# Two attention forms and a phase mixer on one core: paired tails, one more transpose by DMA, copies moved between engines, and a new order of work

## The chip, the cores and the metric

The kernel runs on one core of a Trainium2 chip. The core has TensorE (PE, matrix products), VectorE (DVE), ScalarE (ACT), GpSimd (POOL) and SyncE (SP), which here only issues DMA transfers. The metric is the device time of one execution in microseconds. The kernel before takes 247.88 us as the median of three runs (247.21 to 248.44). The profiled execution has a span of 247.0 us from its first to its last instruction.

## The reference

There are 8 batches, 8 heads, 576 positions and 64 elements per head; the model width is 512. Each batch has an attention over means of four positions, an attention over the seven positions around each one, and then a mixer whose phases come from a product with `w_theta`.

```python
q_d, k_d, v_d = means over 4 neighbouring positions of q, k, v
out_d = softmax(q_d k_d^T / 8) v_d               # 144 x 144, each row repeated 4 times
attn  = softmax(q k^T / 8 where |i - j| < 4)     # 576 x 576, a band
x     = repeat(out_d, 4) + attn v                # then the heads side by side: 576 x 512

theta = x @ w_theta                              # 512 x 512
zr, zi = x * cos(theta), x * sin(theta)
y     = w_tok_r @ zr + w_tok_i @ zi              # 576 x 576, over positions
u     = x + y
out   = u + max(u @ w_ch, 0)                     # 512 x 512
```

## The kernel before

The work of a batch is cut into steps, each a generator, and each step has a letter. The string `ORDER` says in which sequence the program takes them, over all batches; every engine runs its instructions in the order so given. L and v load, C and w cast to bf16, A turns q and k, Q and S form the two kinds of scores, N and V the products with v, T turns the result into xT, H forms the phases, Z multiplies x by cosine and sine, X mixes over positions, R multiplies by `w_ch`, O adds and stores. q, t, x, z and u issue DMA transposes. D are matmuls on zeros that keep TensorE at work.

The 576 positions of a batch are 4 blocks of 128 and a tail of 64.

```python
DMA_QK, DMA_X, DMA_Z = (6, 7), (6, 7), (6, 7)    # batches whose q/k, attention result, x are turned by DMA

def turns(b):                                    # step A; j = q, k, q, k
    for j in range(4):
        if b in DMA_QK:
            ps = turned.pop((b, j)).rearrange("p r w -> p (r w)")      # SBUF, written by a DMA transpose
        else:
            ps = w2(...)                                               # PSUM
            for r in range(WR):                                        # WR = 9
                nc.tensor.transpose(out=ps[:, P * r:P * r + P], in_=tm[:, i, r, :, :], identity=ident)
        for a in range(2):
            act(                                                       # nc.scalar.copy
                out=To[:, 2 * i + a, 0:S].rearrange("p (w r) -> p w r", r=WR),
                in_=ps.rearrange("p (r a w) -> p a w r", r=WR, a=2)[:, a],
            )
        # ... VectorE: tensor_reduce over four positions, to qdT or kdP
```

In these copies the output is written consecutively, and the input is read with a step of 128 elements.

```python
def turn_z(b):                                   # step x
    if b in DMA_Z:
        t = turned[b, "z"] = moep.tile([P, 16, P], BF16, tag="xr", bufs=1, ...)
        nc.sync.dma_start_transpose(out=t, in_=xTs[b][:, 0:4 * MAIN])

def modulate(b):                                 # step Z
    for c in range(4):
        if b in DMA_Z:
            ps = turned[b, "z"][:, c:16:4, :]
        else:
            for dc in range(4):
                nc.tensor.transpose(out=ps[:, dc, :], in_=xA[:, dc, P * c:P * c + P], identity=ident)
        nc.vector.tensor_tensor(out=z[:, 2 * c:2 * c + 2, :]..., in0=ps..., in1=css..., op=ALU.mult)

def mix(b):                                      # step X: psu four times, then psut for the tail
    uT = uTs[b] = moep.tile([P, 4 * S], BF16, tag="uT", ...)
    uA, uB = parted(uT)                          # main blocks and tail in one tile
    for dc in range(4):
        for j in range(9):
            nc.tensor.matmul(out=ps, lhsT=z[:, j, P * dc:P * dc + P], rhs=WT[:, j, 0:MAIN], ...)
        nc.vector.tensor_tensor(out=uA[:, dc, :], in0=ps, in1=xA[:, dc, :], op=ALU.add)
    # ... psut: 36 matmuls of 64 columns, and one addition into uB

def u_turn(b):                                   # step u, twice a batch: ur (main), utr (tail)
    nc.sync.dma_start_transpose(out=ur, in_=uTs[b][:, 0:4 * MAIN])
    nc.sync.dma_start_transpose(out=utr, in_=uTs[b][:, 4 * MAIN:4 * S])

def channels(b):                                 # step R, five times a batch
    # c < 4: four matmuls 128 x 512 into psr; c == 4, the tail of 64 positions:
    for dc in range(4):
        for hf in range(2):
            nc.tensor.matmul(out=psr[64 * hf:64 * hf + 64, 0:256], lhsT=uB[:, dc, :], rhs=wch[...][:, hf], ...)

def store(b):                                    # step O, five times a batch
    osb = moep.tile([P, DM], FP32, tag="osb", bufs=4, ...)
    nc.vector.scalar_tensor_tensor(out=osb..., in0=psr..., scalar=0.0, in1=ur or utr, op0=ALU.max, op1=ALU.add)
    # c < 4: one transfer of 128 rows; c == 4: two transfers of 64 x 2 pieces of 128 floats
```

Four PSUM buffers serve psu, psut, psth, psr and the other small products (`w1`), two larger ones the scores and the products with v (`w2`).

Of the kernel before, what the change touches and what calls it, by code (L numbers as in the profile page):

```python
# [10 lines left out]
BF16 = mybir.dt.bfloat16  # L11
AF = mybir.ActivationFunctionType
ALU = mybir.AluOpType
AX = mybir.AxisListType

P = 128
B = 8
H = 8
S = 576
# [15 lines left out]
WR = 9  # L35
# [6 lines left out]
HALF = 64  # L42
MAIN = 512
# [4 lines left out]
def kernel(  # L48
# [11 lines left out]
    nc = tc.nc  # L60
# [5 lines left out]
    moep = ctx.enter_context(tc.tile_pool(name="moep", bufs=2))  # L66
# [6 lines left out]
    def w2(name, dt=FP32):  # L73
        return ps2.tile([P, 2, 512 if dt == FP32 else 1024], dt, tag="w2" + next(turn2), name=name)

    def w1(name, dt=FP32):
        return ps1.tile([P, 512 if dt == FP32 else 1024], dt, tag="w1" + next(turn1), name=name)


    ORDER = (  # L80
        "LKLLLLLKKCLCCAvCCLvCDwvvvKLCAACwwwwLASCLSVQQCBlLLLLLVSlllllNvlCCCCNlvvvACNVCcScwcvTlTTccllcwAASlHVVH"
        "wwwDTTcAHZHZcHSZcccSDDhLLLzBcCSCWQDVWWLghLLLLCWCCvQvWWLNCNCCWWSWvvLvZNVVXwwwvAAvhwhTXTAALXSwSLLLLXQQ"
        "TBCCVgLggHCuLLVTvHNTVHHZNCCHCCCSwzZZZARRvvvSwOROALSXOLLAAXLLwSwwLvCCCCSCCCCRSNVOXVVXQVTTTAABwSXuTLLA"
        "vvwuvQRvvLLSTSHONNHVLLXuZZANHCLwHwwLVVHRQRRCCCCOzvLLLBOOCCSSTZTCvvRwOTLZSQHVHNVTXTAAXLLACACwCHHwCLCq"
        "LwwqNVHXSZNVXZZvvzSLLCCQCLqXVZLqQvRvwBvOVTVuTTLXTAwASSCHCCHCHNNXqvLwwTwuVXLVLAAHHXqSSZXRQROzONZSCCQC"
        "TCZBSVqROqvvvvZTSSROTVHVRHOTNNTXAAHVHHVwwwwwXAtAXSSzXXSSZZNZVuRuuRRROOQQtOOBRVRVttROtTTTOZOSTNXVRTuN"
        "RRxSSOOOHHVVXtttVHZHZZHNVzZXXttXuXTTXXHTHTTRxROOZHHRuROOHZRZZzOXXXXXXXRuRRRuuOORRuOOROROOORROO"
    )

    staged = {}  # L90
# [86 lines left out]
    for i in range(2):  # L177
        t = const.tile([P, 4, 5, KP], BF16, name=f"kdP{i}")
# [4 lines left out]
    for i in range(2):  # L183
        t = const.tile([P, 4, 5 * 120], BF16, name=f"kT{i}")
# [4 lines left out]
    for i in range(2):  # L189
        t = const.tile([P, NCH, H, 66], BF16, name=f"v_w{i}")  # L190
# [4 lines left out]
    for c in range(NCH):  # L195
        t = const.tile([P, DM], BF16, name=f"tmp{c}")
# [4 lines left out]
    for i in range(2):  # L201
        t = const.tile([P, 2, H, 66], BF16, name=f"vd{i}")
# [7 lines left out]
    dve, act, gp = nc.vector.tensor_copy, nc.scalar.copy, nc.gpsimd.tensor_copy  # L210
# [4 lines left out]
    wch = wpool.tile([P, 4, DM], BF16, name="wch")  # L215
# [69 lines left out]
    parts, turned = {}, {}  # L285


    DMA_QK, DMA_X, DMA_Z = (6, 7), (6, 7), (6, 7)

    def turn_qk(b):  # L290

# [23 lines left out]
    def turns(b):  # L315

        q_tm, k_tm = inputs.pop(b)
        qT = work.tile([P, 4, S], BF16, tag="qT", name=f"qT{b}")
        kT = kTs[b % 2]
        qdT = work.tile([P, 4, SD], BF16, tag="qdT", name=f"qdT{b}")  # L320
        kdP = kdPs[b % 2]
        parts[b] = (qT, kT, qdT, kdP)

        for j in range(4):
            n, i = j % 2, j // 2
            tm, To = ((q_tm, qT), (k_tm, kT))[n]
            if b in DMA_QK:
                ps = turned.pop((b, j)).rearrange("p r w -> p (r w)")
            else:
                ps = w2(f"pstr{n}{i}_{b}", BF16).rearrange("p k e -> p (k e)")[:, 0:WR * P]  # L330
                for r in range(WR):
                    nc.tensor.transpose(out=ps[:, P * r:P * r + P], in_=tm[:, i, r, :, :], identity=ident)  # L332
            for a in range(2):
                act(  # L334
                    out=To[:, 2 * i + a, 0:S].rearrange("p (w r) -> p w r", r=WR),
                    in_=ps.rearrange("p (r a w) -> p a w r", r=WR, a=2)[:, a],
                )
            hs = slice(2 * i, 2 * i + 2)
            dst, src = (qdT[:, hs, :], qT[:, hs, :]) if n == 0 else (kdP[:, hs, :, 0:30], kT[:, hs, :])
            src = src.rearrange("p e (m j) -> p e m j", j=4) if n == 0 else src.rearrange("p e (g m j) -> p e g m j", g=5, j=4)  # L340
            with nc.allow_low_precision(reason="sums are taken in float32 and rounded once"):
                nc.vector.tensor_reduce(out=dst, in_=src, axis=AX.X, op=ALU.add)  # L342
            yield
# [177 lines left out]
    def parted(t):  # L521

        return (t[:, 0:4 * MAIN].rearrange("p (e t) -> p e t", e=4),
                t[:, 4 * MAIN:4 * S].rearrange("p (e t) -> p e t", e=4))
# [85 lines left out]
            yield  # L610


    uTs, urs = {}, {}

    def mix(b):

        (xA, xB), z = parted(xTs[b]), zs.pop(b)
        uT = uTs[b] = moep.tile([P, 4 * S], BF16, tag="uT", name=f"uT{b}")
        uA, uB = parted(uT)
        for dc in range(4):  # L620
            ps = w1(f"psu{dc}_{b}")
            for j in range(9):
                nc.tensor.matmul(out=ps, lhsT=z[:, j, P * dc:P * dc + P], rhs=WT[:, j, 0:MAIN], start=(j == 0), stop=(j == 8))  # L623
            nc.vector.tensor_tensor(out=uA[:, dc, :], in0=ps, in1=xA[:, dc, :], op=ALU.add)  # L624
            yield
        ps = w1(f"psut_{b}")[:, 0:4 * HALF].rearrange("p (e t) -> p e t", e=4)
        for dc in range(4):
            for j in range(9):
                nc.tensor.matmul(out=ps[:, dc, :], lhsT=z[:, j, P * dc:P * dc + P], rhs=WT[:, j, MAIN:S],  # L629
                                 start=(j == 0), stop=(j == 8))  # L630
        nc.vector.tensor_tensor(out=uB, in0=ps, in1=xB, op=ALU.add)
        yield

    def u_turn(b):

        ur = moep.tile([P, 16, P], BF16, tag="ur", name=f"ur{b}")
        utr = moep.tile([P, 2, P], BF16, tag="utr", name=f"utr{b}")
        urs[b] = ur, utr
        nc.sync.dma_start_transpose(out=ur, in_=uTs[b][:, 0:4 * MAIN])
        yield  # L640
        nc.sync.dma_start_transpose(out=utr, in_=uTs[b][:, 4 * MAIN:4 * S])
        yield

    rels = {}

    def channels(b):

        uA, uB = parted(uTs[b])
        for c in range(5):
            psr = rels[b, c] = w1(f"psr{c}_{b}")  # L650
            if c < 4:
                for dc in range(4):
                    nc.tensor.matmul(  # L653
                        out=psr, lhsT=uA[:, dc, P * c:P * c + P], rhs=wch[:, dc, :],
                        start=(dc == 0), stop=(dc == 3),
                    )
            else:

                for dc in range(4):
                    for hf in range(2):  # L660
                        nc.tensor.matmul(  # L661
                            out=psr[64 * hf:64 * hf + 64, 0:256], lhsT=uB[:, dc, :],
                            rhs=wch[:, dc, :].rearrange("p (j e d) -> p e j d", j=2, e=2)[:, hf],
                            start=(dc == 0), stop=(dc == 3),
                        )
            yield

    def store(b):

        ur, utr = urs.pop(b)  # L670
        for c in range(5):
            psr = rels.pop((b, c))
            osb = moep.tile([P, DM], FP32, tag="osb", bufs=4, name=f"osb{c}_{b}")
            n = 4 if c < 4 else 2
            nc.vector.scalar_tensor_tensor(  # L675
                out=osb[:, 0:P * n].rearrange("p (e d) -> p e d", d=P),
                in0=psr[:, 0:P * n].rearrange("p (e d) -> p e d", d=P), scalar=0.0,
                in1=ur[:, c:16:4, :] if c < 4 else utr, op0=ALU.max, op1=ALU.add,
            )
            if c < 4:  # L680
                nc.sync.dma_start(out=out[b, P * c:P * c + P, :], in_=osb)
            else:
                for hf in range(2):
                    nc.sync.dma_start(  # L684
                        out=out[b, 512:576, :].rearrange("t (j e d) -> e t j d", j=2, e=2)[hf],
                        in_=osb[64 * hf:64 * hf + 64, 0:2 * P].rearrange("p (j d) -> p j d", j=2),
                    )
            yield

    last = {}
# [13 lines left out]
    def batches(steps):  # L709
        for b in range(B):  # L710
            yield from steps(b)

    sequences = dict(L=batches(load), v=batches(load_v), C=batches(cast), w=batches(cast_v), A=batches(turns), B=batches(pooled_v), Q=batches(scores), S=batches(band_scores), N=batches(pooled_out), q=batches(turn_qk), t=batches(turn_x), x=batches(turn_z),
                     V=batches(outputs), T=batches(transposes), H=batches(phases), Z=batches(modulate),
                     K=constants(), z=batches(z_turn), u=batches(u_turn), X=batches(mix), R=batches(channels), O=batches(store),
                     l=weight_loads(), c=weight_casts(), h=channel_loads(), g=channel_casts(), W=weight_turns(), D=warm_up())
    pin()
# [35 lines left out]
```

## Time and profile before

| | |
|---|---|
| time, median of 3 | 247.88 us |
| span of the profiled execution | 247.0 us |
| TensorE busy | 224.8 us, 91% |
| VectorE busy | 184.6 us, 75% |
| ScalarE busy | 166.9 us, 68% |
| GpSimd busy | 160.9 us, 65% |
| DMA queue of SyncE, share of 16 engines | 93.3% |
| mean granted clock of TensorE | 0.985 |

A line of the profile's groups names the line of the program, the engine, the operation, output and input by the program's names with partitions x elements, the count, busy time and mean ns of one, and the idle time before them with what ended most of it. Matmuls overlap, so the mean of one is longer than what a further one adds; the chain of waits, which gives the time that a run of matmuls takes on the path, is better for that. A line of the timeline gives start, duration, engine, program line, operation and count.

### The profile page before, as it was taken

To read this page: it belongs to the slowest core of one execution; us is meant where nothing else is said; L and a number is where in the kernel's file an instruction comes from. 1 tells how busy PE (TensorE), PEld (TensorE's weight loads), DVE (VectorE), ACT (ScalarE), POOL (GpSimd) and SP (SyncE) were. 2 spreads that over 40 slices of the span, in tenths; PEclk is the share of its full clock that TensorE was granted. 3 is DMA by queue.
4 is the path that set the end of the run, shared out by engine and by line. 5 is a ranking of instruction groups with operands and counts; after the bars stand their busy time and mean duration, and the time that the engine had idled before them with its cause. 6 is when DMAs were issued, how large, how long until landed. Compare 5 with 4: busy or idle time off the path is not lost. (4 is left out here: it accounts for less than half of the span.)

```text
span 247.0 us, 6608 instructions
## 1 busy us (share of the span) xinstructions
PE 224.8 (91%) x2602; PEld 134.9 (55%) x2602; DVE 184.6 (75%) x345; ACT 166.9 (68%) x248; POOL 160.9 (65%) x223
## 2 busy tenths in 40 slices
PE   0778799999999999999999998999699999999990
PEld 0435465765566566656666555655455655455540
DVE  5274976679879898897989977997687776256462
ACT  3685799766998479988878999899924390250000
POOL 4467485997999999979759664996295942400000
PEclk9997999999999999999999999999989999999999
DMA  6999999999979997999999999599969594946496
GB/s 197 307 272 391 304 211 330 333 224 245 275 200 275 320 197 122 263 239 314 256 185 214 252 184 269 92 172 219 121 156 169 144 209 96 170 160 90 90 262 202
DMA packets 100511, 53.94 MB, mean 218 GB/s; under 512 B 83968, under 2 KB 86016, under 8 KB 100480
## 3 DMA queue, kind: packets, MB, share of 16 engines
q1 hardware_dynamic: 100480, 53.53, 93.3%
q8 instruction: 20, 0.33, 0.6%
q14 instruction: 11, 0.09, 0.2%
HBM read 33.59 MB, written 9.44 MB: 174 GB/s over the span
## 5 line engine op out<-in xcount | busy, mean ns | idle before, releaser
L623 PE MATMUL psu<-WT,z 128*128 128x512 bf16 x288 | 66.3, 379 | 0.5 <-ACT cs L568 0.5
L445 POOL TENSOR_SCALAR_AFFINE_SELECT pm<-pm 128x1024 bf16<-128x1024 bf16 (+1 forms) x35 | 36.6, 1045 | 20.0 <-ACT pm L438 20.0
L438 ACT ACTIVATE pm<-psS 128x1024 bf16<-128x1024 f32 (+1 forms) x40 | 37.7, 979 | 12.7 <-PE psS L430 11.9
L623 PEld LDWEIGHTS <-z 128*128 128x128 bf16 x288 | 26.8, 98 | 29.2 <-issue 0.8
L447 POOL TENSOR_SCALAR_AFFINE_SELECT pm<-pm 128x1024 bf16<-128x1024 bf16 (+1 forms) x35 | 36.6, 1045 | 2.4
L562 PE MATMUL psth<-wth,xT 128*128 128x512 bf16 x128 | 31.5, 379 | 0.1
L624 DVE TENSOR_TENSOR uT<-psu,xT 128x512 bf16<-128x512 f32 x32 | 21.8, 687 | 12.7 <-PE psu L623 12.6
L653 PE MATMUL psr<-wch,uT 128*128 128x512 bf16 x128 | 31.2, 383 | 0.0
L567 ACT ACTIVATE cs<-psth,pihc 128x512 bf16<-128x512 f32 x32 | 22.3, 697 | 11.8 <-PE psth L562 11.3
L131 POOL CAST v_w<-st_v 128x512 bf16<-128x512 f32 (+1 forms) x40 | 23.9, 614 | 9.2 <-DMA st_v<-in_v_dram 9.1
L511 DVE TENSOR_TENSOR tmp<-psloc,rl 120x512 bf16<-120x512 f32 (+2 forms) x40 | 27.6, 691 | 1.4
L342 DVE TENSOR_REDUCE qdT<-qT 128x288 bf16<-128x1152 bf16 x16 | 21.5, 1347 | 8.2 <-ACT qT L334 8.2
L675 DVE SCALAR_TENSOR_TENSOR osb<-psr,ur 128x512 f32<-128x512 f32 x32 | 21.6, 686 | 7.3 <-PE psr L653 6.7
L342 DVE TENSOR_REDUCE kdP<-kT 128x300 bf16<-128x1200 bf16 x16 | 22.3, 1397 | 5.8 <-ACT kT L334 5.8
L124 POOL CAST k_tm<-st_k 128x576 bf16<-128x576 f32 x32 | 21.5, 673 | 4.5 <-DMA st_k<-in_k_dram 4.3
L124 POOL CAST q_tm<-st_q 128x576 bf16<-128x576 f32 x28 | 18.7, 667 | 2.5 <-PE pstr L332 1.3
L334 ACT COPY qT<-pstr 128x576 bf16<-128x576 bf16 x24 | 14.2, 646 | 8.7 <-PE pstr L332 8.7
L545 DVE TENSOR_TENSOR xT<-xTps,xdT 128x480 bf16<-128x480 bf16 (+3 forms) x36 | 18.7, 548 | 0.9 <-PE xTps L541 0.7
L568 ACT ACTIVATE cs<-psth 128x512 bf16<-128x512 f32 x32 | 19.4, 606 | 0.0
L653 PEld LDWEIGHTS <-uT 128*128 128x128 bf16 x128 | 11.5, 99 | 12.2 <-issue 0.8
L430 PE MATMUL psS<-qT,kT 64*128 64x128 bf16 (+1 forms) x320 | 15.0, 220 | 3.1 <-ACT pm L438 2.2
L502 PEld LDWEIGHTS <-pm 128*128 128x128 bf16 (+1 forms) x320 | 14.9, 105 | 5.0 <-issue 0.7
(92 smaller groups left out, 390.2 us busy)
## 6 DMA issues: line engine op xcount, KB each, us to landing
st_q<-in_q_dram SPq DMA_DIRECT2D x32, 288.0 KB, 4.7
st_k<-in_k_dram SPq DMA_DIRECT2D x32, 288.0 KB, 5.0
st_v<-in_v_dram SPq DMA_DIRECT2D x32, 256.0 KB, 5.4
out_dram<-osb SPq DMA_DIRECT2D x32, 256.0 KB, 3.1
st_v<-in_v_dram SPq DMA_DIRECT2D x8, 192.0 KB, 4.8
tok<-in_moe_w_tok_r_dram SPq DMA_DIRECT2D x4, 288.0 KB, 7.6
tok<-in_moe_w_tok_i_dram SPq DMA_DIRECT2D x4, 288.0 KB, 4.2
th<-in_moe_w_theta_dram SPq DMA_DIRECT2D x2, 512.0 KB, 7.1
```

The lines of the kernel that those rows point to most:

```text
L124: eng[i](out=dst[:, hh // 2, :, hh % 2, :], in_=staged.pop((b, f"{'qk'[i]}{hh}")).rearrange("p (r d) -> p r d", d=D))
L131: gp(out=v_ws[b % 2][0:KW[c], c, :, 0:D], in_=staged.pop((b, f"v{c}"))[0:KW[c], 0:DM].rearrange("p (h d) -> p h d", d=D))
L342: nc.vector.tensor_reduce(out=dst, in_=src, axis=AX.X, op=ALU.add)
L438: nc.scalar.activation(out=pv, in_=ps[0:kw].rearrange("p e (j w) -> p (e j) w", w=P)[:, :, 0:qn], func=AF.Exp, scale=SCL,)
L445: nc.gpsimd.affine_select(out=pv, in_=pv, compare_op=ALU.is_ge, fill=0.0, base=off, pattern=[[0, 8], [-1, qn]], channel_multiplier=1)
L447: nc.gpsimd.affine_select(out=pv, in_=pv, compare_op=ALU.is_ge, fill=0.0, base=6 - off, pattern=[[0, 8], [1, qn]], channel_multiplier=-1)
L511: nc.vector.tensor_tensor(out=tmp[0:cnt].rearrange("p (e j d) -> p e j d", e=2, j=4), in0=pv[0:cnt, :, :, 0:D], in1=rl[0:cnt].unsqueeze(3) ...
L562: nc.tensor.matmul(out=th, lhsT=xA[:, dc, P * c:P * c + P], rhs=wth[:, dc, :], start=(dc == 0), stop=(dc == 3),)
L567: nc.scalar.activation(out=cs[:, 0, :], in_=th, func=AF.Sin, bias=pihc, scale=1.0)
L623: nc.tensor.matmul(out=ps, lhsT=z[:, j, P * dc:P * dc + P], rhs=WT[:, j, 0:MAIN], start=(j == 0), stop=(j == 8))
L624: nc.vector.tensor_tensor(out=uA[:, dc, :], in0=ps, in1=xA[:, dc, :], op=ALU.add)
L653: nc.tensor.matmul(out=psr, lhsT=uA[:, dc, P * c:P * c + P], rhs=wch[:, dc, :], start=(dc == 0), stop=(dc == 3),)
```

## The change

It has four parts. The tails of two batches (64 positions each) are put side by side into one tile, so that one block of 128 positions serves both in step R and in the DMA transpose, and one addition on VectorE serves both in step O. Batch 5's x, which TensorE turned for step Z, is turned by DMA as those of batches 6 and 7 are. For batches 6 and 7, whose q and k are turned by DMA, the copies of k go to VectorE, and ScalarE's copies of q run over the elements in the other order: consecutive reads and spaced writes. And the order of the steps is a new one throughout. The aim is to take matmuls off TensorE and copies off ScalarE.

```diff
     ORDER = (
-        "LKLLLLLKKCLCCAvCCLvCDwvvvKLCAACwwwwLASCLSVQQCB...        (694 steps)
+        "KKLLLLCCCCLAALLLvCCvvKCKDwvvLLLCLLLLAALSwwwSwlVVCB...    (683 steps)
     )
 ...
-    DMA_QK, DMA_X, DMA_Z = (6, 7), (6, 7), (6, 7)
+    DMA_QK, DMA_X, DMA_Z = (6,7),(6,7),(5,6,7)
 ...
             for a in range(2):
-                act(
-                    out=To[:, 2 * i + a, 0:S].rearrange("p (w r) -> p w r", r=WR),
-                    in_=ps.rearrange("p (r a w) -> p a w r", r=WR, a=2)[:, a],
-                )
+                dst = To[:, 2 * i + a, 0:S].rearrange("p (w r) -> p w r", r=WR)
+                src = ps.rearrange("p (r a w) -> p a w r", r=WR, a=2)[:, a]
+                if b not in DMA_QK:
+                    act(out=dst, in_=src)
+                elif n == 0:
+                    act(out=dst.rearrange("p w r -> p r w"), in_=src.rearrange("p w r -> p r w"))
+                else:
+                    dve(out=dst, in_=src)
 ...
-        uT = uTs[b] = moep.tile([P, 4 * S], BF16, tag="uT", name=f"uT{b}")
-        uA, uB = parted(uT)
+        uT = uTs[b] = moep.tile([P, 4 * MAIN], BF16, tag="uT", name=f"uT{b}")
+        uA = uT.rearrange("p (e t) -> p e t", e=4)
+        if b % 2 == 0:
+            uBs[b // 2] = moep.tile([P, 4, 2, HALF], BF16, tag="uB", name=f"uB{b // 2}")
+        uB = uBs[b // 2][:, :, b % 2, :]
 ...
+        nc.sync.dma_start_transpose(out=ur, in_=uTs[b])
+        yield
+        if b % 2:
+            utr = utrs[b // 2] = moep.tile([P, 4, P], BF16, tag="utr", name=f"utr{b // 2}")
+            nc.sync.dma_start_transpose(out=utr, in_=uBs[b // 2].rearrange("p e i t -> p (e i t)"))
 ...
-        for c in range(5):
+        for c in range(4 + b % 2):
             psr = rels[b, c] = w1(f"psr{c}_{b}")
+            for dc in range(4):
+                nc.tensor.matmul(
+                    out=psr, lhsT=uA[:, dc, P * c:P * c + P] if c < 4 else uBs[b // 2][:, dc],
+                    rhs=wch[:, dc, :], start=(dc == 0), stop=(dc == 3),
+                )
 ...
-                for hf in range(2):
-                    nc.sync.dma_start(
-                        out=out[b, 512:576, :].rearrange("t (j e d) -> e t j d", j=2, e=2)[hf],
-                        in_=osb[64 * hf:64 * hf + 64, 0:2 * P].rearrange("p (j d) -> p j d", j=2),
-                    )
+                for i in range(2):
+                    nc.sync.dma_start(out=out[b - 1 + i, 512:576, :], in_=osb[HALF * i:HALF * i + HALF])
```

More of the change, by code (lines that the diff above doesn't have):

```diff
@@ L80 @@
     ORDER = (
[L81 to L87, printed above, removed]
+        "KKLLLLCCCCLAALLLvCCvvKCKDwvvLLLCLLLLAALSwwwSwlVVCBClllQQCCvNNllllAANvvvvTSllTSCCccSVHVVCCDlTTcclAccL"
+        "LcTwZwwwwALhHHHcLLLLHSQZZDDQBSDzvLCChWcCCccCCgCScWCNWWSWWvvvwvVWNLWWZwwwwVvALLXAAXVhAhXSSXVNBQTTTggS"
+        "TQHVVHLLLCTCHuLgCCCCCNNLCLLHvvZVHSwXROZzROvvAAZZARALwLLLRCCLwLvvSwwvCvCOSLLOXCCCCSSXVVXAABQNXQVTTSTw"
+        "SuwTTSHVHNNZZLALXAHVNHvwCVHRwQvvuCwwwLLLzLRQRCCOCBSOOZSZTTTARvCCLALwSLHHCvOVXVvLTNLvvLLXTNAHHZZVwwCA"
+        "CCwqXHCCCvvVSXZzZQSXVLLNTBqQCLLqwVTTCLROqAuSSTCvHHVNXTwNCCCLLVAAHHqAHXSSXXXZSZVLqwwvvRRONVSRQzvvOOZS"
+        "TTLQBCCCVqCROTqSZHVVTuXTNwVAwwwHHHxANAAHvSROXXSSwXzQSRRuuOVOZNQXSSBZZZtttRRTOOVVXTRRVRSRttTOTTxONNHO"
+        "OXHVVHHVVttHZZZNZzXXXtttTuXXXTTTHTxHHROROHuRROOZHzZZZROXXXXXXuuRRROOOXuRRRROROOOROO"
     )
@@ L610, in modulate @@
             yield
-    uTs, urs = {}, {}
+    uTs, uBs, urs, utrs = {}, {}, {}, {}
     def mix(b):
         (xA, xB), z = parted(xTs[b]), zs.pop(b)
-        uT = uTs[b] = moep.tile([P, 4 * S], BF16, tag="uT", name=f"uT{b}")
-        uA, uB = parted(uT)
+        uT = uTs[b] = moep.tile([P, 4 * MAIN], BF16, tag="uT", name=f"uT{b}")
[3 more added lines that the diff above has]
+        uB = uBs[b // 2][:, :, b % 2, :]
         for dc in range(4):
@@ L634, in u_turn @@
     def u_turn(b):
[L636 to L639, printed above, removed]
+        ur = urs[b] = moep.tile([P, 16, P], BF16, tag="ur", name=f"ur{b}")
+        nc.sync.dma_start_transpose(out=ur, in_=uTs[b])
         yield
-        nc.sync.dma_start_transpose(out=utr, in_=uTs[b][:, 4 * MAIN:4 * S])
-        yield
+        if b % 2:
+            utr = utrs[b // 2] = moep.tile([P, 4, P], BF16, tag="utr", name=f"utr{b // 2}")
+            nc.sync.dma_start_transpose(out=utr, in_=uBs[b // 2].rearrange("p e i t -> p (e i t)"))
+            yield
@@ L644 @@
     rels = {}
     def channels(b):
-        uA, uB = parted(uTs[b])
-        for c in range(5):
+        uA = uTs[b].rearrange("p (e t) -> p e t", e=4)
+        for c in range(4 + b % 2):
             psr = rels[b, c] = w1(f"psr{c}_{b}")
[L651 to L655, printed above, removed]
-                    )
-            else:
-                for dc in range(4):
-                    for hf in range(2):
[L661 to L665, printed above, removed]
+            for dc in range(4):
[3 more added lines that the diff above has]
+                )
@@ L666, in channels @@
             yield
     def store(b):
-        ur, utr = urs.pop(b)
-        for c in range(5):
+        ur = urs.pop(b)
+        for c in range(4 + b % 2):
             psr = rels.pop((b, c))
             osb = moep.tile([P, DM], FP32, tag="osb", bufs=4, name=f"osb{c}_{b}")
-            n = 4 if c < 4 else 2
             nc.vector.scalar_tensor_tensor(
-                out=osb[:, 0:P * n].rearrange("p (e d) -> p e d", d=P),
-                in0=psr[:, 0:P * n].rearrange("p (e d) -> p e d", d=P), scalar=0.0,
-                in1=ur[:, c:16:4, :] if c < 4 else utr, op0=ALU.max, op1=ALU.add,
+                out=osb.rearrange("p (e d) -> p e d", d=P),
+                in0=psr.rearrange("p (e d) -> p e d", d=P), scalar=0.0,
+                in1=ur[:, c:16:4, :] if c < 4 else utrs.pop(b // 2), op0=ALU.max, op1=ALU.add,
@@ L682, in store @@
             else:
-                for hf in range(2):
-                    nc.sync.dma_start(
-                        out=out[b, 512:576, :].rearrange("t (j e d) -> e t j d", j=2, e=2)[hf],
-                        in_=osb[64 * hf:64 * hf + 64, 0:2 * P].rearrange("p (j d) -> p j d", j=2),
-                    )
+                for i in range(2):
+                    nc.sync.dma_start(out=out[b - 1 + i, 512:576, :], in_=osb[HALF * i:HALF * i + HALF])
             yield
```

## The prediction

> **What bounds the kernel now.** I read the views in this order: the busy shares of the page, the windows of 10 us, the waits of TensorE, the timeline around the longest late wait, the groups kept apart by shape, and the timeline of the end. The first line that matters is the busy share:
>
> ```profile
> PE 224.8 (91%) x2602; PEld 134.9 (55%) x2602; DVE 184.6 (75%) x345; ACT 166.9 (68%) x248; POOL 160.9 (65%) x223
> ```
>
> TensorE is busy for 224.8 of 247.0 us, so 22.2 us are its idle time. The windows tell where those 22.2 us lie (columns: length, then busy us and instruction count of PE, PEld, DVE, ACT and POOL, the granted clock, the DMA share, GB/s):
>
> ```profile
> 0.00:10.00 10.00, 3.08 (x15) 1.70 (x16) 4.32 (x37) 4.73 (x8) 4.18 (x15) 1.00 0.80 253
> 10.00:20.00 10.00, 7.68 (x91) 4.15 (x89) 6.08 (x8) 7.91 (x13) 5.68 (x11) 0.89 1.10 282
> 20.00:30.00 10.00, 7.44 (x105) 5.13 (x105) 7.02 (x12) 6.00 (x10) 6.64 (x10) 0.94 1.08 352
> ...
> 130.00:140.00 10.00, 10.00 (x123) 6.10 (x121) 9.86 (x19) 9.04 (x11) 7.51 (x12) 1.00 1.21 239
> 140.00:150.00 10.00, 9.51 (x122) 5.65 (x121) 7.63 (x14) 9.98 (x15) 6.22 (x9) 1.00 1.24 199
> 150.00:160.00 10.00, 9.10 (x132) 5.60 (x130) 8.48 (x17) 8.77 (x13) 8.14 (x10) 1.00 0.81 181
> 160.00:170.00 10.00, 10.00 (x106) 5.95 (x104) 8.57 (x16) 9.99 (x14) 9.59 (x12) 1.00 1.03 182
> 170.00:180.00 10.00, 7.78 (x103) 5.12 (x102) 7.07 (x12) 9.79 (x11) 3.71 (x5) 0.91 0.94 153
> 180.00:190.00 10.00, 10.00 (x109) 5.64 (x107) 7.70 (x15) 3.35 (x6) 8.33 (x10) 0.92 0.74 165
> ```
>
> Of the idle time, 6.9 + 2.3 + 2.6 = 11.8 us lie in the first 30 us, where inputs arrive. The end takes about 5.5 us after the last matmul. Between 140 and 180 us 0.5 + 0.9 + 2.2 = 3.6 us are lost, and there ScalarE is busy 9.98, 8.77, 9.99 and 9.79 of every 10 us. That is the stretch of batches 6 and 7, whose q and k are turned by DMA. After the 2.2 us of idleness the granted clock is 0.91 and 0.92 for two windows. The timeline there shows the cause:
>
> ```profile
> 170.43 2.37 ACT L334 COPY qT<-qk 128x576 bf16<-128x576 bf16 x2
> 172.63 2.36 ACT L334 COPY kT<-qk 128x576 bf16<-128x576 bf16 x2
> 175.01 1.28 ACT L438 ACT_TABLE_LOAD   x1
> ```
>
> TensorE then waits 1.92 us for the exponentials behind that table load (psS from pm, at 177.38). ScalarE's copies of turned q and k stand directly on the path. Their price is in the groups by shape (busy us, mean ns):
>
> ```profile
> L334 ACT COPY kT<-pstr 128x576 bf16<-128x576 bf16 x24 | 14.3, 656 | 2.8 <-PE pstr L332 2.7
> L334 ACT COPY qT<-qk 128x576 bf16<-128x576 bf16 x8 | 9.3, 1237 | 0.0
> L334 ACT COPY kT<-qk 128x576 bf16<-128x576 bf16 x8 | 9.3, 1232 | 0.0
> L247 DVE CAST wtm<-tok 128x576 bf16<-128x576 f32 x4 | 1.6, 452 | 0.0
> ```
>
> The same copy of 576 elements takes 656 ns out of PSUM and 1232 ns out of SBUF.
>
> **What the Trainium skill says.** "SBUF — State Buffer", Specifications, says that SBUF has lines of 16 bytes, that at least two accesses should fall in a line, and that each crossing has a price. The copies from qk read bf16 elements 256 bytes apart, one per line; the trace agrees in direction (1237 against 656 ns, though the second reads PSUM). A consecutive read of float32 from SBUF, the cast of q, takes 675 ns on ScalarE, which points the same way. "VectorE: DVE Perf Modes", section What auto-detection actually checks, says that a one-source operation with both operands in SBUF and an even outermost dimension may run at two elements a cycle without unit step. The k copy has an outermost dimension of 64, so it qualifies; the trace has only a consecutive example, the cast above at 452 ns. "SBUF — State Buffer", section Who interferes with whom, adds that such a two-port operation and a GpSimd operation shut each other out; no run here shows that yet. "ScalarE: Activation LUTs", section What ACT_TABLE_LOAD costs, gives 1283 ns a load; the trace has 1283 ns.
>
> **The change, part by part.**
>
> *Batch 5's x by DMA.* 16 transposes leave TensorE (4 blocks by 4). In the chain of waits a group of four takes 0.22 us at full clock, so 4 x 0.22 = 0.9 us. I don't use the group's mean of 231 ns, which is latency of one; they overlap. VectorE's product is as long from SBUF (683 ns) as from PSUM (682 ns). One DMA transpose of 4.3 us is added. The build places it ahead of the last x of batch 5's users by more than two mixing steps of 1.94 us of TensorE, so I take it as hidden.
>
> *Tails of two batches.* Before, each batch has 8 matmuls of 256 columns, 0.56 us in the chain: two batches 1.12 us. After, four of 512 columns serve both, 0.86 us. Four pairs save 4 x 0.26 = 1.0 us. VectorE does 4 x 686 ns in place of 8 x 418: 0.6 us less. The tail stores fall from 16 to 8, each of 64 rows of 2 KB.
>
> *k to VectorE, q with consecutive reads.* ScalarE loses 8 x 1.232 = 9.9 us (9.3 busy, overlaps taken out). If the q copies fall to the 0.66 us of the other copies, another 8 x 0.58 = 4.6 us go. VectorE gains 8 copies of k. I estimate 0.45 us (the two-element rate) to 0.75 us (576 elements at 0.96 GHz as implied by the reduction of 1152 in 1347 ns, with 150 ns fixed); 0.6 x 8 = 4.8 us. ScalarE so loses 14 us, exactly in the stretch where it is 88 to 100% busy. What TensorE can win is at most the 3.6 us of waits plus the lost clock: 20 us at 0.915 less the idle 2.2 us, about 1.5 us. So 5 us at most. VectorE is 76% to 99% busy there, so not all of it comes back; I count 2.2 us.
>
> *The end.* Let T be the end of the last full mixing step of batch 7 (232.28 in the chain). Before, 1.05 us of tail mixing, eight products of 0.86 and two of 0.56 follow, so TensorE ends at T + 9.1. VectorE then waits for output buffers:
>
> ```profile
> 238.65 0.43 DVE L675 SCALAR_TENSOR_TENSOR osb<-psr,utr 128x256 f32<-128x256 f32 x1 [1.13 <-DMA out_dram<-osb]
> ...
> 241.96 0.69 DVE L675 SCALAR_TENSOR_TENSOR osb<-psr,ur 128x512 f32<-128x512 f32 x1 [0.38 <-DMA out_dram<-osb]
> 242.79 0.42 DVE L675 SCALAR_TENSOR_TENSOR osb<-psr,utr 128x256 f32<-128x256 f32 x1
> ```
>
> It all ends at T + 14.7. After, three products come ahead of the tail mixing, and there are nine results in place of ten. TensorE ends at 3 x 0.86 + 1.05 + 6 x 0.86 = T + 8.8. The turned u of batch 7 is issued at T + 0.8 and takes 5.3 us, so batch 7's four results run on VectorE from T + 6.1 at 0.69 us each. The last one needs the buffer of the first of them: 6.8 + 0.4 of issue + 2.2 of landing = T + 9.4. Then 0.7 of VectorE, two issues of 0.6 and about 2.5 of landing: T + 13.8. Gain 0.9 us, in which the fourth pair's 0.26 us is contained.
>
> *The new order.* In the first 30 us it puts the loads of a whole batch ahead of v, does both first turns before the warm-up matmuls, and the first two products of v ahead of the rest. Walking it by hand with the durations above, the first score block ends near 15 us as before. TensorE then idles longer for the pooled scores, but has less to wait for later. I count 0.3 us gained, with an error of over 1 us.
>
> Sum: 0.9 (x) + 0.8 (three pairs) + 2.2 (waits and clock at 140 to 190) + 0.9 (end) + 0.3 (start) = 5.1 us. 247.9 - 5.1 = 242.8; because the new order was presumably arranged for the shorter copies I shade it to 242.4.
>
> **Rivals.** *VectorE becomes the bound.* It is 9.86 us busy in 130 to 140 and does four copies for each of two batches more. If a strided read also costs it double, a copy takes some 1.3 us, 10 us in all, into a stretch of 50 us with about 9 us free: the wait on ScalarE turns into one on VectorE and the time is 245 to 247. Against it speaks that VectorE falls to 5.8 busy of 10 after 220 us and the order can shift work there. *The work leaves TensorE but its waits stay.* All transfers go through one queue in order, x of three batches shares one buffer, and the paired tail holds back an even batch's last result until the odd batch is mixed. If those or the start give new waits, only the 1.7 us of matmuls plus the end are left: 244.5 to 246. *Everything is regained.* If the stretch at 140 to 190 gives all 5 us and the start 1.5 us, it is near 238.5. For this speaks that ScalarE is the only engine TensorE waits for there.
>
> **Range and chances.** The certain part is about 2.6 us (matmuls and end); the rest goes from -1 to 6.5 us. That gives 239.0 to 246.0. Two per cent is 242.9, just above my middle: faster 0.55, within 2% 0.40, slower 0.05.
>
> **What would show it.** Copies of q near 660 ns and of k at 450 to 750 ns; no wait of TensorE for pm behind such copies; a granted clock near 1.0 at 170 to 190; TensorE busy near 223 us; the end about 13.8 us after the last full mixing step. Wrong if k copies take over 1.2 us, if TensorE gets new waits for VectorE or a DMA, or if the first 30 us lose more than 13 us.

## The result, and the profile after

| | before | after |
|---|---|---|
| time, median of four runs | 248.09 us (247.21 to 248.44) | 255.78 us (255.27 to 256.3) |
| ratio, 95% interval | | 1.0315, 1.0278 to 1.0353 |
| span of the profiled execution | 247.0 us | 254.6 us |
| TensorE's mean granted clock | 0.985 | 0.967 |

The kernel became 3% slower; 242.4 us and a range up to 246.0 us had been predicted. The page's busy shares after:

```profile
PE 227.2 (89%) x2538; PEld 134.9 (53%) x2538; DVE 191.8 (75%) x349; ACT 169.8 (67%) x240; POOL 162.4 (64%) x223
```

TensorE has the 64 instructions less that were meant. ScalarE, which was to lose 14 us, has 2.9 us more, although eight copies left it. The groups by shape say why (busy us, mean ns):

```profile
L339 ACT COPY qT<-qk 128x576 bf16<-128x576 bf16 x8 | 21.4, 2934 | 0.0
...
L609 DVE TENSOR_TENSOR z<-xr,cs 128x1024 bf16<-128x1024 bf16 x12 | 10.1, 890 | 0.0
...
L341 DVE COPY kT<-qk 128x576 bf16<-128x576 bf16 x8 | 4.8, 648 | 0.0
```

A q copy now takes 2934 ns, where it took 1237. For all eight that is 12.1 us more of busy time, against 9.3 us that left with k, which leaves 2.8 of the 2.9 us. The k copies on VectorE take 648 ns. The windows show where TensorE pays (columns as in the prediction):

```profile
130.00:140.00 10.00, 6.91 (x104) 4.42 (x101) 6.74 (x13) 9.64 (x10) 6.67 (x10) 0.94 1.05 253
140.00:150.00 10.00, 9.82 (x88) 5.24 (x87) 7.80 (x14) 9.99 (x11) 5.96 (x8) 0.89 1.06 201
...
170.00:180.00 10.00, 7.12 (x67) 3.75 (x65) 4.68 (x6) 10.00 (x10) 2.95 (x5) 1.00 0.96 192
180.00:190.00 10.00, 7.00 (x57) 3.27 (x56) 7.61 (x12) 6.38 (x10) 6.77 (x8) 0.83 0.48 54
```

ScalarE (fourth pair) is full in 130 to 150 and 170 to 180. TensorE (first pair) is idle for 3.1 us in the first of these windows, and for 2.9 and 3.0 us in the last two; the clock is 0.94, 0.89 and 0.83 in the first, the second and the last of the four. ScalarE's timeline (start, duration) at the second place:

```profile
174.84 5.30 ACT L339 COPY qT<-qk 128x576 bf16<-128x576 bf16 x2
179.61 0.74 ACT L583 ACTIVATE cst<-pstt,pihc 128x256 bf16<-128x256 f32 x1
180.21 0.41 ACT L584 ACTIVATE cst<-pstt 128x256 bf16<-128x256 f32 x1
180.63 1.28 ACT L442 ACT_TABLE_LOAD   x1
181.93 2.67 ACT L442 ACTIVATE pm<-psS 128x1024 bf16<-128x1024 f32 x3
```

It is the picture of before, only that a pair of copies takes 5.30 us instead of 2.37. The exponentials come behind it, and TensorE's waits (us in total, times, longest) name them:

```profile
PE psS L434 <- ACT pm L442: 4.7, 1, 4.7
PE psloc L506 <- ACT pm L442: 3.7, 4, 2.8
```

The end did not get shorter. The last full mixing step of batch 7 ends at 239.50 and the span at 254.6, which is T + 15.1; it was T + 14.7, and T + 13.8 was predicted. On VectorE the last results still wait for output buffers:

```profile
246.75 1.96 DVE L671 SCALAR_TENSOR_TENSOR osb<-psr,ur 128x512 f32<-128x512 f32 x3 [2.02 <-DMA out_dram<-osb]
249.19 0.69 DVE L671 SCALAR_TENSOR_TENSOR osb<-psr,ur 128x512 f32<-128x512 f32 x1 [0.48 <-DMA out_dram<-osb]
```

### The profile page after: what moved, and what is told of

Read it like the earlier page. It is cut to its first block, busy times and chain, and to the rows that moved or that the text cites. A ratio compares the mean times of both kernels' runs of the same rounds, so it can differ in the third digit from the quotient of the medians.

```text
span 254.6 us, 6457 instructions
## 1 busy us (share of the span) xinstructions
PE 227.2 (89%) x2538; PEld 134.9 (53%) x2538; DVE 191.8 (75%) x349; ACT 169.8 (67%) x240; POOL 162.4 (64%) x223
## 4 chain that ended last, share of the span: by engine, by line
PE 73%; ACT 15%; DVE 4%; DMA 3%; issue 3%; SPq 1%; DVEq 0%; ACTq 0%
PE psu L630 21%; PE psth L566 10%; PE psr L659 9%; PE pstr L332 4%; PE psloc L506 4%; PE psS L434 4%; PE psut L636 3%; ACT pm L442 3%; PE xTps L545 3%; ACT qT L337 2%; ACT kT L337 2%; PE wu L277 2%; PE psnd L468 2%; DMA st_q<-in_q_dram 2%; ACT qT L339 2%
## 5 line engine op out<-in xcount | busy, mean ns | idle before, releaser
L630 PE MATMUL psu<-WT,z 128*128 128x512 bf16 x288 | 68.8, 390 | 0.6 <-DVE z L609 0.4
L449 POOL TENSOR_SCALAR_AFFINE_SELECT pm<-pm 128x1024 bf16<-128x1024 bf16 (+1 forms) x35 | 37.4, 1070 | 27.3 <-ACT pm L442 27.1
L630 PEld LDWEIGHTS <-z 128*128 128x128 bf16 x288 | 27.6, 100 | 32.6 <-issue 3.9
L451 POOL TENSOR_SCALAR_AFFINE_SELECT pm<-pm 128x1024 bf16<-128x1024 bf16 (+1 forms) x35 | 37.0, 1057 | 2.4
L571 ACT ACTIVATE cs<-psth,pihc 128x512 bf16<-128x512 f32 x32 | 22.8, 713 | 12.1 <-PE psth L566 10.4
L124 POOL CAST k_tm<-st_k 128x576 bf16<-128x576 f32 x32 | 21.5, 671 | 5.5 <-DMA st_k<-in_k_dram 4.8
L339 ACT COPY qT<-qk 128x576 bf16<-128x576 bf16 x8 | 21.4, 2934 | 0.0
L434 PE MATMUL psS<-qT,kT 64*128 64x128 bf16 (+1 forms) x320 | 15.1, 217 | 5.3 <-ACT pm L442 4.7
L506 PE MATMUL psloc<-v_w,pm 128*128 128x65 bf16 (+1 forms) x320 | 16.5, 197 | 3.7 <-ACT pm L442 3.7
L506 PEld LDWEIGHTS <-pm 128*128 128x128 bf16 (+1 forms) x320 | 14.7, 103 | 8.7 <-issue 3.4
```

The source lines that it names most:

```text
L124: eng[i](out=dst[:, hh // 2, :, hh % 2, :], in_=staged.pop((b, f"{'qk'[i]}{hh}")).rearrange("p (r d) -> p r d", d=D))
L339: act(out=dst.rearrange("p w r -> p r w"), in_=src.rearrange("p w r -> p r w"))
L434: nc.tensor.matmul(out=ps[0:kw, par, P * hh:P * hh + qn], lhsT=kT[64 * par:64 * par + 64, hh, KS[c]:KS[c] + kw], rhs=qT[64 * par:64 * par ...
L449: nc.gpsimd.affine_select(out=pv, in_=pv, compare_op=ALU.is_ge, fill=0.0, base=off, pattern=[[0, 8], [-1, qn]], channel_multiplier=1)
L451: nc.gpsimd.affine_select(out=pv, in_=pv, compare_op=ALU.is_ge, fill=0.0, base=6 - off, pattern=[[0, 8], [1, qn]], channel_multiplier=-1)
L506: nc.tensor.matmul(out=pv[0:qn, h // 4, h % 4, :], lhsT=pms[b][c][0:kw, 4 * par + blk, 0:qn], rhs=v_w[0:kw, c, h, 0:65], start=(h % 4 == 0 ...
```

## The experiments

Two things were to be settled: what makes the q copy slow and whether it alone is the loss, and why the rest of the change brings so little. Ratios are to the kernel before, with their 95% intervals. Each expectation says itself what its theories hold.

**The q copy taken back.** The changed kernel with ScalarE's q copies read and written as before.

```diff
-                    act(out=dst.rearrange("p w r -> p r w"), in_=src.rearrange("p w r -> p r w"))
+                    act(out=dst, in_=src)
```

> The changed kernel with one thing undone: ScalarE's copies of turned q read with a step and write consecutively again. Theory A (the spaced writes cost the loss): the copies fall from 2.93 to about 1.24 us, ScalarE loses 8 x 1.7 = 13.6 us of busy time, TensorE's waits of 2.8 and 4.7 us for pm go, and the time is 243 to 247 us. Rival B (the new order, or batch 5's x by DMA, costs the loss): the copies fall as well but the time stays at 251 us or above.

Measured: 246.17 us, ratio 0.9952 (0.9928 to 0.9975); q copies 1218 ns. The longest wait of TensorE for pm falls from 4.7 to 0.6 us. So this one line costs 0.036 x 248 = 9 us, more than the whole loss. What is left gains half a per cent where 2% was predicted. The windows of before and then of this kernel, 20 us each, show what took ScalarE's place:

```profile
150.00:170.00 20.00, 19.10 (x233) 11.55 (x232) 17.05 (x32) 18.75 (x26) 17.73 (x21) 1.00 0.92 182
170.00:190.00 20.00, 17.78 (x209) 10.76 (x208) 14.77 (x26) 13.14 (x17) 12.04 (x14) 0.91 0.84 159
```

```profile
150.00:170.00 20.00, 19.69 (x242) 11.93 (x242) 19.45 (x37) 15.83 (x22) 17.68 (x22) 1.00 0.90 206
170.00:190.00 20.00, 18.32 (x199) 9.64 (x198) 19.83 (x28) 10.77 (x15) 15.89 (x16) 1.00 0.81 142
```

VectorE (third pair) goes from 17.05 and 14.77 to 19.45 and 19.83 of 20 us. TensorE's idle time in 130 to 190 us falls only from 3.6 to 2.95 us. Before, it was all spent in waits for ScalarE; now the two largest waits in that stretch are for VectorE (us in total, times, longest):

```profile
PE psu L630 <- DVE z L609: 1.0, 2, 0.9
PE psxt L608 <- DVE uT L631: 0.8, 1, 0.8
```

VectorE's timeline there has batch 5's products from x in SBUF:

```profile
180.58 1.62 DVE L609 TENSOR_TENSOR z<-xr,cs 128x1024 bf16<-128x1024 bf16 x1
...
182.46 4.23 DVE L609 TENSOR_TENSOR z<-xr,cs 128x1024 bf16<-128x1024 bf16 x3
```

Four products take 5.85 us, where four of 0.68 us would take 2.7. GpSimd's masks beside them grow as well. The one that starts with the first product keeps its 1.09 us, one of the later ones does not:

```profile
180.57 1.09 POOL L449 TENSOR_SCALAR_AFFINE_SELECT pm<-pm 128x1024 bf16<-128x1024 bf16 x1
...
183.11 1.54 POOL L449 TENSOR_SCALAR_AFFINE_SELECT pm<-pm 128x1024 bf16<-128x1024 bf16 x1
```

**The q copy alone, on the kernel before.**

```diff
+                if b not in DMA_QK or n == 1:
+                    act(out=dst, in_=src)
+                else:
+                    act(out=dst.rearrange("p w r -> p r w"), in_=src.rearrange("p w r -> p r w"))
```

> The kernel before with one part of the change: ScalarE's copies of turned q read consecutively and write spaced; k stays on ScalarE, the order is the old one. Theory A: copies of about 2.9 us, 13.6 us more on a ScalarE that is already full between 140 and 180 us; the time rises by 7 to 13 us to 255 to 261 us. Rival B: the time rises by less than 3 us.

Measured: 260.6 us, ratio 1.0502 (1.0454 to 1.0551), and one wait of TensorE for pm of 4.6 us. The copies:

```profile
L339 ACT COPY qT<-qk 128x576 bf16<-128x576 bf16 x8 | 21.5, 2956 | 0.0
```

The line does its harm without the other parts: the q copies keep ScalarE busy for 21.5 in place of 9.3 us, 12.2 us more, and the time grows by 12.4 us.

**Reads and writes apart.** In the changed kernel ScalarE's q copies of batches 6 and 7 read and write consecutively (the reordering of q is left out there), and VectorE's k copies read consecutively and write 18 bytes apart.

```diff
-                    act(out=dst.rearrange("p w r -> p r w"), in_=src.rearrange("p w r -> p r w"))
+                    act(out=To[:, 2 * i + a, 0:S].rearrange("p (r w) -> p r w", r=WR), in_=src.rearrange("p w r -> p r w"))
                 else:
-                    dve(out=dst, in_=src)
+                    dve(out=dst.rearrange("p w r -> p r w"), in_=src.rearrange("p w r -> p r w"))
```

> A probe, not a version: ScalarE copies turned q with consecutive reads and consecutive writes, which leaves the reordering of q in batches 6 and 7 out; VectorE copies turned k with consecutive reads and spaced writes. If the spaced writes alone make ScalarE's copies 2.93 us, they fall to 0.65 to 0.7 us here; if the long second dimension does, they stay above 2 us. If VectorE pays for spaced writes as ScalarE does, k copies go from 0.65 us to above 1.5 us; if not, they stay below 0.8 us.

The one run took 254.61 us. Its groups:

```profile
L341 DVE COPY kT<-qk 128x576 bf16<-128x576 bf16 x8 | 13.9, 1925 | 0.0
...
L339 ACT COPY qT<-qk 128x576 bf16<-128x576 bf16 x8 | 5.0, 692 | 0.0
```

On ScalarE the same 576 elements take 692 ns with both sides consecutive, 1218 to 1237 with reads 256 bytes apart, and 2934 with writes 18 bytes apart. The copies of 692 and of 2934 ns run over the elements in the same order, so the order is not what makes them slow. On VectorE reads apart cost 648 ns and writes apart 1925 on average; part of the latter is GpSimd's work beside them, and the pair during which GpSimd was nearly idle took 2.99 us, some 1.5 us each. On both engines the spaced write costs by far the most. What VectorE needs with both sides consecutive was not measured.

**The prediction's premise granted.** As the last one, for q only; k stays as changed. The reordering of q in batches 6 and 7 is left out.

```diff
-                    act(out=dst.rearrange("p w r -> p r w"), in_=src.rearrange("p w r -> p r w"))
+                    act(out=To[:, 2 * i + a, 0:S].rearrange("p (r w) -> p r w", r=WR), in_=src.rearrange("p w r -> p r w"))
```

> The changed kernel with one line altered: ScalarE's q copies of batches 6 and 7 read and write consecutively (qT is laid out with the 128-position pieces one after the other, so the reordering of q is left out there and the output is not the reference's). It grants the prediction its premise: q near 0.69 us, k on VectorE near 0.65 to 0.75 us. Theory P (the sum of the prediction was right but for the size of the q copy): 242 to 243.5 us, ratio 0.977 to 0.982, no TensorE wait over 1 us between 130 and 190 us. Theory V (VectorE is the bound there whatever ScalarE's copies cost): as with the old copies of q, 245.5 to 247 us, ratio 0.992 to 0.998, VectorE over 19 of 20 us busy at 150 to 190 and ScalarE idle for longer there. I hold V for more likely, since with the old copies ScalarE was already busy for only 44 of the 60 us from 130 to 190 us and VectorE for 58.

Measured: 245.73 us, ratio 0.9922 (0.9901 to 0.9943). The copies were what the prediction had put into its sum, q 693 ns and k 726 ns, and still it gains 0.8% and not 2.1%. The last window of 20 us:

```profile
170.00:190.00 20.00, 18.28 (x208) 9.77 (x209) 19.83 (x29) 9.19 (x13) 18.38 (x17) 1.00 0.72 153
```

VectorE has 19.83 of 20 us, as much as with q copies of 1218 ns, and ScalarE falls to 9.19. The interval overlaps that of the first experiment (0.9928 to 0.9975): a further shortening of ScalarE buys next to nothing.

**k on VectorE alone, on the kernel before.**

```diff
+                if b not in DMA_QK or n == 0:
+                    act(out=dst, in_=src)
+                else:
+                    dve(out=dst, in_=src)
```

> The kernel before with one part of the change: turned k copied by VectorE, q by ScalarE as before, old order. Theory A: k copies of 0.65 us on VectorE, 9.3 us less on ScalarE, the wait of 1.92 us behind the copies of batch 7 goes: 244.5 to 247 us. Rival C (VectorE has no room there): 248 us or more.

Measured: 247.96 us, ratio 1.0014 (0.9993 to 1.0035). VectorE is busy 19.73 and 19.18 of 20 us in 130 to 170, and its k copies take 964 ns on average. ScalarE is freed of 8.4 us and nothing comes of it: the wait has changed engines. The two largest waits of TensorE from 130 to 190 us are now

```profile
PE psxt L606 <- DVE uT L626: 1.2, 1, 1.2
PE psS L432 <- DVE tmp L513: 1.0, 1, 1.0
```

**q on VectorE too.** The changed kernel, all copies of turned q and k on VectorE.

```diff
-                    act(out=dst.rearrange("p w r -> p r w"), in_=src.rearrange("p w r -> p r w"))
+                    dve(out=dst, in_=src)
```

> The changed kernel with q copied by VectorE too, in the way of k. Theory A: 8 copies of about 0.65 us on VectorE, none on ScalarE, 242 to 245 us, at or a little under the first kernel of this call. Rival C (VectorE becomes the bound between 130 and 190 us): 246 us or more, with waits of TensorE on VectorE in place of those on ScalarE. Rival B: 251 us or above.

Measured: 253.37 us, ratio 1.0235 (1.0199 to 1.027). I had expected a gain and was wrong. The q copies average 1146 ns there. A pair takes 1.22 us while GpSimd rests, but this beside GpSimd's casts and masks:

```profile
134.88 3.89 DVE L339 COPY qT<-qk 128x576 bf16<-128x576 bf16 x2
```

TensorE then waits 3.7 us for k and 2.7 us for a product of VectorE. That is the prediction's first rival (VectorE becomes the bound) in its full form.

**Batch 5's x back on TensorE**, the q copies as before (from here on every kernel is built on that of the first experiment unless another is named). Step x of batch 5 is also dropped from `ORDER`.

```diff
-    DMA_QK, DMA_X, DMA_Z = (6,7),(6,7),(5,6,7)
+    DMA_QK, DMA_X, DMA_Z = (6,7),(6,7),(6,7)
```

> The changed kernel with ScalarE's q copies as before (stepped reads) and batch 5's x turned by TensorE again. In the run with the q copies alone undone, the four products z<-xr of batch 5 took 5.85 us in all on a VectorE that is 99% busy there, while GpSimd worked; from PSUM they take 0.68 us each. Theory D (a product with two SBUF inputs is held up by GpSimd): they fall to 2.7 us though GpSimd works as before, VectorE gains 3.1 us, TensorE pays 0.9 us for 16 transposes, and the time is 243.5 to 245.5 us. Rival E (the place in the order, not the source, makes them slow): they stay above 1 us each and the time is 246.5 us or more.

Measured: 246.91 us, ratio 0.9982 (0.9953 to 1.0012). At the same place in the order, with GpSimd as busy, batch 5's products out of PSUM take 0.68 us each, two of them here:

```profile
181.95 1.29 DVE L609 TENSOR_TENSOR z<-psxt,cs 128x1024 bf16<-128x1024 bf16 x2 [0.79 <-PE psxt L608]
```

VectorE falls from 19.83 to 16.72 of 20 us. But the 16 transposes are back on TensorE and wait for their PSUM buffer (1.4 us for ScalarE), while TensorE had waited only 1.0 us for the slow products. What makes the products slow is shown, and a gain isn't: x by DMA and x by TensorE cost about the same here. So a VectorE that is busy for 19.83 of 20 us isn't shown to set the time by itself; that wait of 1.0 us tells more of what the slow products cost than the busy share does.

**No masks.** GpSimd's two masks of the exponentials are left out for batches 5 to 7, so the scores outside the window count there.

```diff
-            if not masked:
+            if not masked and b < 5:
```

> The changed kernel with the q copies as before, and GpSimd's two masks on the exponentials left out for batches 5 to 7, so that their local attention is over more than the band. GpSimd is then nearly idle from 140 us on. Theory D (GpSimd and VectorE hold each other up): the products z<-xr of batch 5 fall from 1.5 to 0.68 us, the k copies from 0.76 to 0.60 to 0.65 us, zT from 0.74 to about 0.45 us, VectorE loses 4 to 5 us of busy time between 130 and 190 us, and the time falls by 2 to 4 us. Rival (they are slow for another reason): the durations stay and the time falls by less than 1 us.

Measured: 243.92 us, ratio 0.9844 (0.9799 to 0.989). The groups:

```profile
L609 DVE TENSOR_TENSOR z<-xr,cs 128x1024 bf16<-128x1024 bf16 x12 | 7.6, 685 | 0.1
...
L341 DVE COPY kT<-qk 128x576 bf16<-128x576 bf16 x8 | 5.6, 743 | 0.0
```

The products fall from 955 to 685 ns, all twelve. The k copies stay at 743, against what I expected; the timeline has the reason: the slow pair (1.98 us from 144.60) lies beside casts of GpSimd, of which one takes 1.05 instead of 0.61 us, and the pairs at 140.77 and 166.16, with GpSimd at rest, take 1.22 us. VectorE's busy time in 130 to 190 falls by 2.2 us (57.96 to 55.73), half of what I expected, and TensorE's idle time to 1.3 us. This run also takes away work on the path from the exponentials to the products with v, so not all of its gain is the contention's.

**The order.** The kernel with x of batch 5 on TensorE, in the order of the kernel before.

> The code of the first kernel of this call (paired tails, k on VectorE, q as before, x of batches 6 and 7 by DMA) in the old order, from which only the steps that pairing drops are taken out. Theory G (the new order is what gains): 246.5 to 248.5 us, 2 us or more over the first kernel. Rival (the order is neutral, the parts gain): within 0.7 us of the first kernel.

Measured: 247.24 us, ratio 0.9976 (0.9942 to 1.001), against 0.9982 in the new order. The edit is the list of steps alone. The new order neither gains nor loses that can be measured.

**The end: one store earlier.** The kernel with x of batch 5 on TensorE in the new order, with one result of batch 6 (its product and store) put ahead of the last transposes.

```diff
-...HROROHuRROOZHzZZZROXXXXXXuuRRROOOXuRRRROROOOROO
+...HROROHuRROOZHzZZZROXXXXXXuuRRROOOXROuRRRROROOOROO
```

> As the kernel before it in this call, but at the end the result R6.3/O6.3 comes ahead of the DMA transpose of the last tails in the order, so that its store is issued before that transpose. Theory F (the store waits behind the transpose in the one DMA queue and so holds the output buffers): the second wait of VectorE for an output buffer goes and the end shortens by 0.5 to 1.5 us. Rival: the end is bound by the turned u of batch 7 (4.5 us after its issue) or the transpose of the tails, and the time is the same within 0.3 us.

Measured: 246.64 us, ratio 0.9971 (0.9946 to 0.9996), end at T + 14.65 instead of T + 14.7. It doesn't matter.

**The end: seven output buffers**, first on the changed kernel with the old q copies, then on the kernel before.

```diff
-            osb = moep.tile([P, DM], FP32, tag="osb", bufs=4, name=f"osb{c}_{b}")
+            osb = moep.tile([P, DM], FP32, tag="osb", bufs=7, name=f"osb{c}_{b}")
```

> The changed kernel with the q copies as before (stepped reads) and 7 output buffers in place of 4. Theory H (the end is held by output buffers: the first store of the last nine takes up to 4.4 us beside the last DMA transpose of u): VectorE's waits of 2.0 and 0.45 us for buffers go, the end falls from 15.0 us after the last full mixing step to 13 to 14 us, and the time is 244 to 245.5 us. Rival (the end is bound by the turned u or by the queue of transfers): the end stays at 14.5 to 15 us and the time at 246 us.

> The kernel before with 7 output buffers in place of 4. Theory H: its waits of 1.1, 0.4 and 0.2 us for buffers at the end go, and the time falls by 0.5 to 1.5 us, to 246 to 247 us. Rival: no change within 0.3 us.

Measured: 245.57 us, ratio 0.9882 (0.983 to 0.9933), end at T + 14.2, and on the kernel before 246.82 us, ratio 0.9962 (0.9941 to 0.9983), T + 13.8. VectorE's waits for buffers at the end are gone in both. In the first, the chain then ends in the two transposes by DMA (start, duration):

```profile
230.56 4.02 DMA ur<-uT
234.58 4.07 DMA utr<-uB
```

They follow one another, so the four blocks of batch 7 and the paired tail can't come sooner. The first of the two kernels is the best version found. It is faster than the kernel before by 1.2%, and its interval doesn't meet that of the second. It does meet that of the first experiment (0.9928 to 0.9975), so what the buffers add there isn't settled by its six runs.

## Why the prediction was wrong

**The step that failed** is that of the copies: "If the q copies fall to the 0.66 us of the other copies, another 8 x 0.58 = 4.6 us go". They rose to 2.93 us. I had taken the price of 1237 ns for that of the reads and left the writes of 18 bytes' step at nothing; the copies out of PSUM, from which I took the 656 ns, are no model for it: they read spaced and write consecutively. The page of the Trainium skill that the prediction rests on, "SBUF — State Buffer", section Specifications, speaks of lines and of a price for each crossing and doesn't separate reads from writes; I had applied it to the reads alone. The direction for reads was right (1237 against 692 ns); with the writes spaced it is 2934. Taking the line back gives 9 us, and having it alone costs 12.4 us, so this is shown to be the cause of the loss. No rival named it: all of them varied where the work goes, none the size of this copy, and the list of what would show the prediction wrong had a limit for k copies and none for q.

**With that size put right, the sum is still too high.** The premise granted, 0.0078 x 248 = 1.9 us came out of 5.1.

- *x off TensorE, paired tails*: TensorE's busy time fell by 2.8 us (224.8 to 222.0) in the first experiment. Multiplied by the mean granted clock (0.985 and 0.989) these are 221.4 and 219.6 us, so my estimate of the work taken off is 1.8 us, where 0.9 + 1.0 were predicted; that part held. But "VectorE's product is as long from SBUF (683 ns) as from PSUM (682 ns)" was read from batches 6 and 7, whose eight products in the kernel before ran at 201 to 206 and 217 to 225 us, while GpSimd's last mask ended at 200.4 and no other of its work lay beside them. Batch 5's came to lie beside the masks and took 1.46 us each. The Trainium skill, "SBUF — State Buffer", section Who interferes with whom, says that a VectorE instruction with two inputs in SBUF contends with a GpSimd instruction that reads SBUF; I had applied the section to the k copy only. The traces agree: products with one source in PSUM keep 0.68 us beside masks, those with both in SBUF keep it only without them.
- *k to VectorE*: 0.648 us in the changed kernel, inside 0.45 to 0.75. In the first experiment it was 0.761. On the kernel before it was 0.964: two pairs of 1.21 us, and two of 2.13 and 2.81 us beside GpSimd's masks and casts.
- *Waits and clock at 140 to 190*: I counted 2.2 us. Of TensorE's idle time in 130 to 190 us 0.7 us came back in the first experiment. The clock rose there from 0.97 to 1.00, but these are one execution of each. The execution that I had read took 248.78 us at a mean clock of 0.985; 31 executions of the same kernel beside the first experiment had medians of 247.49 us and 0.992, and the 20 of the first experiment 0.988. So the clock, about 1.5 us of the 5 us that I had put as the most, was in part a property of the execution that I happened to read, and no gain in clock is shown. The first rival (VectorE becomes the bound) is right in so far as TensorE's waits moved to VectorE, though for a reason that it didn't have: the copy isn't slow by its strided reads, but by contention and by coming on top of an engine that was busy for 71 to 99% of the windows from 130 to 190 us (I had read 76: the window from 170 to 180 has 7.07 of 10 us).
- *The end*: 0.9 us predicted, none found (T + 15.1; T + 15.0 with the old q copies). I had let a store land 2.2 us after its issue. With four buffers VectorE waits 2.0 us for one, as the stores move beside the transposes of u and take up to 4.4 us to land; with seven buffers those waits are gone, and the second transpose behind the first is the limit. On the kernel before the same buffers give T + 13.8 against T + 14.2, so in these two profiles the paired tail doesn't shorten the end.
- *The order*: 0.3 predicted with an error of over 1 us; not measurable.

What stays open: how the missing 3.2 us divide exactly. My estimate from the one profile with the premise granted: TensorE's idle time at 130 to 190 us fell by 0.9 us (3.6 to 2.7) where 2.2 were counted, and the end took T + 14.9 where T + 13.8 was predicted, which makes 1.3 + 1.1 = 2.4 of the 3.2. Smaller waits from 30 to 130 us may be in it too (TensorE idle 1.2 us before, 1.8 in the first experiment). One profile of each kernel can't separate terms of half a microsecond while its executions lie 3 us apart. Batch 5's products with x by DMA at a place without masks weren't tried.

## What to carry to other kernels

A copy that reorders has one side spaced: measure which side is dear before turning it round, on the engine that will do it and with both sides as they will be. Before counting lost clock as a gain, look at the clock of more than one execution. Before moving work to another engine, look at that engine in the same 20 us and not over the span, and at who works beside it there: a duration read where GpSimd rests isn't the one that will hold where it works. And where a cost is uncertain in both directions, give "it gets dearer" a rival of its own.

## What the runs showed of the hardware

- A copy of 576 bf16 elements with writes 18 bytes apart: 2.93 us on ScalarE, and on VectorE 1.93 on average and some 1.5 with GpSimd nearly idle; with reads 256 bytes apart and consecutive writes 1.23 and 0.65; ScalarE with both consecutive 0.69.
- VectorE and GpSimd lengthen one another: a product of 1024 elements from two SBUF sources 0.68 us alone and 1.4 to 1.6 beside masks, the masks 1.09 us alone and 1.4 to 1.5 beside it. With one source in PSUM the product stays at 0.68.
